# The first sequence of a spectral-mixing and SwiGLU kernel, by a written list of steps over eight PSUM banks

## The chip, the cores and the metric

The kernel runs on one core of a Trainium2 chip. The metric is the device time of one launch in microseconds; lower is better. The core has a matrix engine (PE, TensorE), three engines for elementwise work (DVE is VectorE, ACT is ScalarE, POOL is GpSimd), a fast memory (SBUF), eight banks of accumulators that PE writes (PSUM), and DMA queues. Each engine takes its instructions in the order in which they were written. In this kernel the queue of SP holds the intermediate stores, transposes and output stores, and the queue of POOL holds the loads of inputs and weights, between POOL's own arithmetic.

## The reference

Eight sequences of 3008 tokens with 256 channels are filtered in the frequency domain, and every token then goes through a normalised gated feed-forward layer:

```python
X = np.fft.rfft(x, axis=1)
Y = X * (filt_r + 1j * filt_i)[None]
y = np.fft.irfft(Y, n=3008, axis=1).reshape(-1, 256)
rms = np.sqrt(np.mean(y * y, axis=-1, keepdims=True) + 1e-06)
xn = y / rms * rms_g
g = xn @ w_gate                    # 256 x 1536
val = xn @ w_val
out = (g * (1 / (1 + np.exp(-g))) * val) @ w_out   # 1536 x 256
```

Inputs and output are float32; the kernel works with 16-bit floats in the matrix products.

## The kernel before

The transform of length 3008 = 47 * 64 is split in two matrix stages. For each sequence there are these steps, and each is a handful of matrix products into one PSUM bank followed by one instruction that moves the bank to SBUF:

- A (`a_unit`; `a0_unit` for the first sequence): the transform over 64. It needs a quarter of x (`x_load(b, c)`, four loads of six token groups each).
- B (`b_unit`): the transform over 47, sixteen units of 4 frequencies by 128 channels. Unit number 2g + dh holds frequencies 4g to 4g + 3 and channel half dh.
- The products with the filter (`s_part`): two per unit, both on DVE. The one with e = 0 multiplies by the real part of the filter, the one with e = 1 by the imaginary part, of which one half must have been negated before. Unit i needs the negated piece of its own four frequencies and its own channel half.
- The inverse transform over 47 (`bi_unit`), and over 64 (`n_unit`), the normalisation, and for each of 6 groups of 512 tokens twelve steps of the feed-forward layer (`gv` and `down`).

Sequences 1 to 7 are prepared while PE works on the feed-forward layer of the sequence before; a planner at the end of the function puts their steps into the slots between `gv` calls. The first sequence has nothing to hide behind. Its part, from the first line under `tc.manual_schedule()` to `first_norm()`, is the prologue, and the change is there. In it the filter must also be turned (`f_unit(i, f, dh)`: four 32-bit transposes and two copies into the table `ff`; i is which of three staged tiles of filter rows, f = 0 the imaginary and f = 1 the real part, dh the channel half), the A results are transposed on PE (`tr0_unit(g)`, one copy of 96 x 1024), and the products are turned and added on PE (`yt0_unit`, one copy of 96 x 512). `f_neg(k0, n, dhs)` on POOL writes the negated imaginary part for n frequencies from k0 on, `f_last` one special column. Everything is issued in program order on each engine.

Four staging tiles (the pool `stg`) hold, one after the other, the three tiles of filter rows `fst[0..2]`, the three tiles of gate and value weights (`w_load(q)`, two DMAs of 512 KB each, called `ws`) and later the tiles y. With four buffers, `w_load(0)` gets the fourth; `w_load(1)` and `w_load(2)` each need a tile of filter rows whose transposes are over. `w_load(0)` and `w_load(1)` stand at the front of POOL's list, before any `f_neg`. `w_gain(q)` on POOL scales the staged weights by `moe_rms_g` into `wg` and `wv`; `wo_load(q)` loads a third of `w_out`. Third q of the weights serves the feed-forward steps jt = 4q to 4q + 3.

Before the change the sixteen units run in a loop of one unit per turn, in the order `od`: B of one unit, its two products, the turning (`yt0_unit`) of a unit two places earlier, the inverse (`bi_unit`) of one four places earlier. B uses the banks mx and mb in turn, the turning the two buffers of psG and the inverse the two of psV. All eight `tr0_unit` copies are on DVE, all twelve `f_unit` copies on ACT, and nearly all turning and inverse copies on ACT.

After the loop come two A units of the second sequence, a small first group of transposes and the first normalisation (`t4_first`, `first_norm`), and four transposing DMAs of all of the first sequence on SP's queue (`t4_load`). A tiny copy on POOL, `seen`, waits for the second of these, and holds back the loads that stand behind it.

Of the kernel before, what the change touches and what calls it, by code (L numbers as in the profile page):

```python
# [1 line left out]

# [1 line left out]

# [16 lines left out]
P = 128  # L21
D = 256
B = 8
# [3 lines left out]
K2 = 32  # L27
# [74 lines left out]
def kernel(  # L102
# [31 lines left out]
    xnp = ctx.enter_context(tc.tile_pool(name="xnp", bufs=4))  # L134
    hp = ctx.enter_context(tc.tile_pool(name="hp", bufs=4))
    op = ctx.enter_context(tc.tile_pool(name="op", bufs=2))
    psG = ctx.enter_context(tc.tile_pool(name="psG", bufs=2, space=bass.MemoryType.PSUM))
    psV = ctx.enter_context(tc.tile_pool(name="psV", bufs=2, space=bass.MemoryType.PSUM))
    psO = ctx.enter_context(tc.tile_pool(name="psO", bufs=1, space=bass.MemoryType.PSUM))
    psM = ctx.enter_context(tc.tile_pool(name="psM", bufs=1, space=bass.MemoryType.PSUM))  # L140
    psB = ctx.enter_context(tc.tile_pool(name="psB", bufs=1, space=bass.MemoryType.PSUM))
# [44 lines left out]
            nc.gpsimd.dma_start(t.rearrange("p a d -> p (a d)"), src(N2, XC))  # L186
        st[b]["x"][c] = t

    def bank(i, name):
        pool, tag = ((psM, "mx"), (psG, "pg"), (psV, "pv"), (psB, "mb"), (psO, "po0"))[i]  # L190
        return pool.tile([P, 512], FP32, tag=tag, name=name)

    def copy(eng, out, in_, scale=None):
        if eng == "A":
# [16 lines left out]
        nc.sync.dma_start(dst, st[b]["t1"][c])  # L211

    def t2_tile(b, c):
        if b == 0 and c == 3:
            st[b]["t2"][c] = op.tile([KR, KC, D], FP16, tag="o3", name="t2o")
        else:
            st[b]["t2"][c] = t2p.tile([KR, KC, D], FP16, tag="t2", name="t2")
# [5 lines left out]
    def s_part(b, i, e, eng=None):  # L223
        eng = eng or nc.vector
        g, dh = divmod(i, 2)
        ps, s = st[b]["s"][i]
        fv = ff[:, dh, 4 * g:4 * g + 4, :]
        o = s[e].rearrange("p k (r q) -> p k r q", r=2)
        if e == 0:
            f1 = fv[:, :, 2 * SL:3 * SL].unsqueeze(2).to_broadcast([P, 4, 2, SL])  # L230
            eng.tensor_tensor(out=o, in0=ps, in1=f1, op=ALU.mult)  # L231
        else:
            f2 = fv[:, :, 0:2 * SL].rearrange("p k (r q) -> p k r q", r=2)
            eng.tensor_tensor(out=o, in0=ps[:, :, ::-1, :], in1=f2, op=ALU.mult)  # L234

    def b_unit(b, i, bk=3, e=0):
        g, dh = divmod(i, 2)
        ps = bank(bk, "psb")[:, 0:4 * KR]
        for k in range(4):
            kk = 4 * g + k  # L240
            nc.tensor.matmul(ps[:, ts(k, KR)], st[b]["t2"][kk // KC][:, kk % KC, ds(dh * P, P)],  # L241
                             wb[0:KR, kk, :], start=True, stop=True)
# [119 lines left out]
    def tr0_unit(g, eng):  # L362
        pool, tag = ((psO, "po0"), (psO, "po1"), (psM, "mx"))[g % 3]
        ps = pool.tile([KR, 4, 2, P], FP16, tag=tag, name="pst")
        for k in range(4):
            for dh in range(2):
                nc.tensor.transpose(ps[:, k, dh, :], va[:, dh, 4 * g + k, :], ident)  # L367
# [17 lines left out]
    def f_unit(i, f, dh, e):  # L385
        t = fst[i]
        ps = bank(1 + "AV".index(e), "psf").rearrange("p (a q) -> p a q", a=FR4)
        for a in range(FR4):
            nc.tensor.transpose(ps[:, a, :], t[:, f, a, ds(dh * P, P)], idf)  # L389
# [17 lines left out]
    def f_neg(k0, n, dhs=(0, 1)):  # L407
        for dh in dhs:
            nc.gpsimd.tensor_scalar(out=ff[:, dh, k0:k0 + n, 0:SL], in0=ff[:, dh, k0:k0 + n, SL:2 * SL],
                                    scalar1=-1.0, scalar2=1.0, op0=ALU.mult, op1=ALU.mult)  # L410

    def yt0_unit(i, eng, bk, ks=slice(0, 4)):
        g, dh = divmod(i, 2)
# [119 lines left out]
    def gv(b, m, jt):  # L533
        n = nq(b, m)
        xn = st[b]["xn"][m]
        parts = ((0, 2), (2, 4)) if (b, m, jt) in SPLIT else ((0, n),)
        sg = hp.tile([P, 512], FP16, tag="sg", name="sg")
        hh = hhs[(6 * JT * b + JT * m + jt) % 4]
        made = []
        for q0, q1 in parts:  # L540
            w = (q1 - q0) * P
            pg = psG.tile([P, 512], FP32, tag="pg", name="pg")
            pv = psV.tile([P, 512], FP32, tag="pv", name="pv")
            for ps, wt in ((pg, wg), (pv, wv)):
                for dt_ in range(2):
                    nc.tensor.matmul(ps[:, 0:w], wt[:, dt_, ts(jt, P)], xn[:, q0:q1, dt_, :],  # L546
                                     start=(dt_ == 0), stop=(dt_ == 1))
# [49 lines left out]
    def wo_load(q):  # L597
        nc.gpsimd.dma_start(wo[:, ts(q, JT // 3), :],
                            moe_w_out.rearrange("(jt p) d -> p jt d", p=P)[:, ts(q, JT // 3), :])

    def w_gain(q):
        cols = ts(q, DFF // 3)
        t = wst.pop(q)
        for k, dst in enumerate((wg, wv)):
            for dt_ in range(2):
                nc.gpsimd.tensor_scalar(out=dst[:, dt_, cols], in0=t[:, k, dt_, :],
                                        scalar1=gsb[:, dt_:dt_ + 1], scalar2=1.0,
                                        op0=ALU.mult, op1=ALU.mult)

    with tc.manual_schedule():  # L610
        nc.vector.memset(ss3[0], 0.0)
# [61 lines left out]
        f_unit(1, 1, 1, "A")  # L673
        f_unit(2, 0, 1, "A")
        b_unit(0, od[2], 4, 1)
        f_unit(2, 1, 0, "A")
        for p in range(3):
            s_part(0, od[p], 0)
        for p in range(UN + 3):
            if 3 <= p < UN:  # L680
                b_unit(0, od[p], (0, 3)[p % 2])
                s_part(0, od[p], 1)
            if p == 0:
                f_unit(2, 1, 1, "A")
                f_neg(4, 12, (1,))
                f_last()
                f_neg(0, 4)
                w_load(2)
                wo_load(0)
                f_neg(16, 16)  # L690
# [5 lines left out]
            if 2 <= p < UN + 1:  # L696
                yt0_unit(od[p - 2], "A", 1)
            if p == UN + 1:
                yt0_unit(UN - 1, "V", 1, slice(0, 2))
                yt0_unit(UN - 1, "A", 0, slice(2, 4))  # L700
            if 4 <= p < UN + 3:
                bi_unit(0, od[p - 4], "AV"[p == UN + 1], 2)
            if UN + 1 <= p < UN + 3:
                fill(1, 1)
        bi_unit(0, UN - 1, "V", 3, slice(0, 2))
        bi_unit(0, UN - 1, "A", 0, slice(2, 4))
        a_unit(1, 0, "A", 1)
        t4_first()
        a_unit(1, 1, "V", 0)
        fill(1, 3)  # L710
        for c in range(NXC):
            t4_load(0, c)
        nc.gpsimd.tensor_copy(out=seen, in_=st[0]["t4"][1][:, 0, 0:4])
# [171 lines left out]
```

## Time and profile before

| | before |
|---|---|
| median of 3 runs | 863.09 us (863.01 to 863.34) |
| the profiled execution's own time | 863.15 us |
| its span in the trace | 861.4 us |
| PE busy | 852.4 us (99%) |
| DVE / ACT / POOL busy | 557.2 / 612.4 / 297.8 us |
| granted TensorE clock | 0.999 |
| first `gv` product on PE | 43.38 us after the span's start |

In the rows below, the first number is the start in microseconds from the span's start, the second the length of the group, then engine, line, operation, output and input, the count, and in brackets the idle time before it with what ended it. Instructions of one engine overlap a little: a product of 0.55 us on DVE is followed by the next one after 0.465 us. Two steps of a group (x2) are shown as one row.

### The profile page before, as it was taken

What the parts mean: (1) busy time and instruction counts of PE and PEld (TensorE: products, weight loads), DVE (VectorE), ACT (ScalarE), POOL (GpSimd) and SP (SyncE); (2) the same over time, 40 slices, a digit from 0 to 9 for tenths busy, and PEclk for the clock granted to TensorE, in tenths of its full rate; (3) what the DMA queues carried; (4) which work ended last, traced back from release to release, by engine and by line L of the source; (5) the groups of instructions that cost most, each with busy time, mean ns of one, the idle gap of its engine ahead of it and who ended that gap; (6) DMA issues with size and microseconds to landing.
All of it is one profiled execution on the core that took longest, in us unless ns stands there. A gap on an engine that the chain in (4) does not pass through costs nothing.

```text
span 861.4 us, 17024 instructions
## 1 busy us (share of the span) xinstructions
PE 852.4 (99%) x6142; PEld 532.2 (62%) x6142; DVE 557.2 (65%) x926; ACT 612.4 (71%) x1339; POOL 297.8 (35%) x346
## 2 busy tenths in 40 slices
PE   8999999999999999999999999999999999999997
PEld 6755666566666666666666666666666666665664
DVE  5857655776666666666666676767666665555554
ACT  4986777787588756887577856888567765777443
POOL 5725742453144322534034430444123430132000
PEclk9999999999999999999999999999999999999999
DMA  9995778765975476656755548433564331521101
GB/s 283 270 204 124 150 164 168 139 130 121 197 137 129 121 150 111 151 107 147 139 127 113 132 98 180 108 87 101 131 127 93 97 70 42 124 54 49 62 25 50
DMA packets 198237, 107.98 MB, mean 125 GB/s; under 512 B 158566, under 2 KB 182520, under 8 KB 198152
## 3 DMA queue, kind: packets, MB, share of 16 engines
q1 hardware_dynamic: 189464, 85.52, 44.1%
q0 software_dynamic: 8544, 21.24, 12.7%
q8 instruction: 48, 0.79, 0.4%
q14 instruction: 37, 0.30, 0.1%
q10 hardware_dynamic: 144, 0.13, 0.0%
HBM read 45.78 MB, written 35.65 MB: 95 GB/s over the span
## 4 chain that ended last, share of the span: by engine, by line
PE 96%; DMA 1%; ACT 1%; DVE 1%; issue 0%; POOL 0%; POOLq 0%
PE po L563 28%; PE pg L546 28%; PE pv L546 28%; PE psb L241 3%; PE psi L285 3%; PE psn L314 2%; PE psa L206 2%; DMA fs<-in_filt_i_dram 1%; PE psy L418 1%; PE psf L389 1%; PE pst L367 0%; ACT sg L550 0%; POOL xc L186 0%; DVE s L231 0%; DVE hh L551 0%
## 5 line engine op out<-in xcount | busy, mean ns | idle before, releaser
L551 DVE TENSOR_TENSOR hh<-pv,sg 128x512 f16<-128x512 f32 (+2 forms) x578 | 391.5, 678 | 286.4 <-ACT sg L550 221.9
L550 ACT ACTIVATE sg<-pg 128x512 f16<-128x512 f32 (+2 forms) x578 | 337.4, 584 | 217.6 <-PE pg L546 213.4
L546 PE MATMUL pg<-xn,wg 128*128 128x512 f16 (+2 forms) x1156 | 338.1, 374 | 0.1
L546 PE MATMUL pv<-xn,wv 128*128 128x512 f16 (+2 forms) x1156 | 338.1, 374 | 0.0
L563 PE MATMUL po<-wo,hh 128*128 128x256 f16 x2256 | 332.7, 273 | 0.0
L563 PEld LDWEIGHTS <-hh 128*128 128x128 f16 x2256 | 213.4, 98 | 105.5 <-issue 0.6
L268 POOL TENSOR_TENSOR ss<-s,s 128x384 f16<-128x384 f16 x112 | 101.9, 911 | 273.2 <-DVE s L234 245.2
L546 PEld LDWEIGHTS <-wv 128*128 128x128 f16 x1156 | 112.9, 98 | 130.7
L546 PEld LDWEIGHTS <-wg 128*128 128x128 f16 x1156 | 111.4, 98 | 17.0 <-issue 0.3
L340 POOL TENSOR_TENSOR xt<-y,rho 128x1024 f16<-128x1024 f32 (+1 forms) x46 | 85.4, 1856 | 2.8
L322 ACT ACTIVATE junk<-y 128x256 f16<-128x256 f32 x180 | 74.3, 413 | 2.8
L231 DVE TENSOR_TENSOR s<-psb,ff 128x384 f16<-128x384 f32 x124 | 67.6, 547 | 0.7 <-ACT ff L195 0.6
L234 DVE TENSOR_TENSOR s<-psb,ff 128x384 f16<-128x384 f32 x124 | 67.6, 546 | 0.0
L195 ACT ACTIVATE uu<-psi 128x384 f16<-128x384 f32 (+1 forms) x127 | 61.6, 486 | 1.5 <-DMA out_dram<-o 0.5
L195 ACT ACTIVATE y<-psn 128x512 f32<-128x512 f32 (+1 forms) x95 | 55.7, 588 | 4.2
L285 PEld LDWEIGHTS <-yt 96*128 96x128 f16 x512 | 35.4, 97 | 26.7 <-issue 1.0
L332 POOL TENSOR_TENSOR rho<-u,mhalf 128x4 f32<-128x4 f32 (+1 forms) x46 | 46.5, 1010 | 3.8
L330 POOL TENSOR_SCALAR u<-ss 128x4 f32<-128x4 f32 (+1 forms) x46 | 8.9, 193 | 104.8 <-ACT junk L322 103.8
L195 ACT ACTIVATE t<-psa 128x512 f16<-128x512 f32 x70 | 41.4, 594 | 3.1 <-PE psa L206 1.7
L285 PE MATMUL psi<-wi,yt 96*128 96x96 f16 x512 | 42.9, 205 | 0.1
L241 PE MATMUL psb<-wb,t 96*128 96x96 f16 x480 | 40.1, 206 | 0.3 <-DVE s L234 0.2
L241 PEld LDWEIGHTS <-t 96*128 96x128 f16 x480 | 28.7, 97 | 12.8 <-DVE s L234 3.3
(101 smaller groups left out, 366.2 us busy)
## 6 DMA issues: line engine op xcount, KB each, us to landing
out_dram<-o SPq DMA_DIRECT2D x40, 512.0 KB, 3.6
xc<-in_x_dram POOLq DMA_DIRECT2D x31, 384.0 KB, 5.6
z_tmp<-t SPq DMA_DIRECT2D x28, 384.0 KB, 2.7
t<-z_tmp SPq DMA_DIRECT2D x28, 384.0 KB, 6.0
out_dram<-o SPq DMA_DIRECT2D x7, 384.0 KB, 2.7
fs<-in_filt_i_dram POOLq DMA_DIRECT2D x3, 512.0 KB, 10.8
fs<-in_filt_r_dram POOLq DMA_DIRECT2D x3, 512.0 KB, 11.2
ws<-in_moe_w_gate_dram POOLq DMA_DIRECT2D x3, 512.0 KB, 9.8
```

The lines of the kernel that those rows point to most:

```text
L195: nc.scalar.activation(out=out, in_=in_, func=AXT.Copy, **({} if scale is None else {"scale": scale}))
L231: eng.tensor_tensor(out=o, in0=ps, in1=f1, op=ALU.mult)
L234: eng.tensor_tensor(out=o, in0=ps[:, :, ::-1, :], in1=f2, op=ALU.mult)
L241: nc.tensor.matmul(ps[:, ts(k, KR)], st[b]["t2"][kk // KC][:, kk % KC, ds(dh * P, P)], wb[0:KR, kk, :], start=True, stop=True)
L268: nc.gpsimd.tensor_tensor(out=ss3[g % 3][:, :, dh, 0:KR], in0=s[0], in1=s[1], op=ALU.add)
L285: nc.tensor.matmul(ps[:, k, :], yt[0:KR, k, dh, :], wi[0:KR, 4 * g + k, :], start=True, stop=True)
L322: nc.scalar.activation(out=junk, in_=y[:, i, ts(u, D)], func=AXT.Square, accum_out=ss[:, 2 * i + u:2 * i + u + 1])
L340: nc.gpsimd.tensor_tensor(out=xt[:, 0:n, :], in0=y.rearrange("p a (u d) -> p (a u) d", u=2)[:, 0:n, :], in1=rho[:, 0:n].unsqueeze(2).to_br ...
L546: nc.tensor.matmul(ps[:, 0:w], wt[:, dt_, ts(jt, P)], xn[:, q0:q1, dt_, :], start=(dt_ == 0), stop=(dt_ == 1))
L550: nc.scalar.activation(out=sg[:, c], in_=pg[:, 0:w], func=AXT.Silu)
L551: nc.vector.tensor_tensor(out=hh[:, c], in0=pv[:, 0:w], in1=sg[:, c], op=ALU.mult)
L563: nc.tensor.matmul(po[s4 // 2][:, s4 % 2, :], hh[:, ts(s4, P)], wo[:, jt, :], start=(jt == 0 and s4 % 2 == 0), stop=(jt == JT - 1 and (s4 ...
```

## The change

- **Banks.** The tags of psG and psV become two tags with one buffer each (`pg0`, `pg1`, `pv0`, `pv1`), so that each step of the prologue can name any of the eight banks. The feed-forward steps still alternate between the two of each kind.
- **A written list.** The loop over units is replaced by the string `STEPS`. Each entry is one step and its bank. F is `f_unit` (three digits i, f, dh, and then the engine of its copies), T is `tr0_unit` (g and the engine), N is `f_neg` for 4 frequencies (dh and g), L is `f_last`, B is a unit's transform (`b0_unit`), P is one product (unit and e), Y is the turning, I the inverse, W, O, X and G are loads and weight scaling, Z a filler product.
- **Order.** The filter tile 0 is turned half at first (F001, F000) and its second half late (F010 in the middle, F011 last). The first five products of the list are imaginary ones (P6.1, P2.1, P3.1, P5.1, P4.1), which need negated pieces; before, the first three were imaginary ones also. Some copies change engine: those of T1, T2 and T5 move to ACT, those of F100, F010, Y13 and I10 to DVE, and that of I14 to ACT.
- **Six product buffers** in place of four: the two more are the tiles `hh0` to `hh3`.
- **Negation in sixteen pieces** of 4 frequencies and one channel half, each an instruction of 192 elements, in place of seven larger ones.
- **Loads.** `w_load(2)` stands after thirteen of the sixteen negated pieces; `x_load(1, 0)` and `x_load(1, 1)` stay in the prologue. `wo_load(1)`, `x_load(1, 2)` and `x_load(1, 3)` move behind `seen`, ahead of `wo_load(2)`. `w_gain` is called by halves (gate, value): three halves in the list, two more after `t4_load`, the last after the loads.

```diff
-    psG = ctx.enter_context(tc.tile_pool(name="psG", bufs=2, space=bass.MemoryType.PSUM))
-    psV = ctx.enter_context(tc.tile_pool(name="psV", bufs=2, space=bass.MemoryType.PSUM))
+    psG = ctx.enter_context(tc.tile_pool(name="psG", bufs=1, space=bass.MemoryType.PSUM))
+    psV = ctx.enter_context(tc.tile_pool(name="psV", bufs=1, space=bass.MemoryType.PSUM))
...
+    BANKS = {"mx": (psM, "mx"), "mb": (psB, "mb"), "o0": (psO, "po0"), "o1": (psO, "po1"),
+             "g0": (psG, "pg0"), "g1": (psG, "pg1"), "v0": (psV, "pv0"), "v1": (psV, "pv1")}
...
     def t2_tile(b, c):
-        if b == 0 and c == 3:
+        if b == 0 and len(st[b]["t2"]) == 3:
...
+    def b0_unit(i, bk, soft):
+        g, dh = divmod(i, 2)
+        ps = bank(bk, "psb")[:, 0:4 * KR]
+        for k in range(4):
+            kk = 4 * g + k
+            nc.tensor.matmul(ps[:, ts(k, KR)], st[0]["t2"][kk // KC][:, kk % KC, ds(dh * P, P)],
+                             wb[0:KR, kk, :], start=True, stop=True)
...
+        st[0]["s"][i] = (ps.rearrange("p (k r q) -> p k r q", k=4, r=2), s0_free.pop(0))
...
-    def w_gain(q):
+    def w_gain(q, k):
         cols = ts(q, DFF // 3)
-        t = wst.pop(q)
-        for k, dst in enumerate((wg, wv)):
-            for dt_ in range(2):
...
-        todo = [(i, f, dh) for i in range(2) for f in range(2) for dh in range(2)][:7] + [(2, 0, 0)]
-        for u in todo[0:2]:
-            f_unit(*u, "A")
-        for g in range(7):
-            tr0_unit(g, "V")
-            if g < 6:
-                f_unit(*todo[g + 2], "A")
-        f_neg(4, 4, (0,))
-        f_neg(8, 8, (0,))
-        UN = K2 // 2
-        od = [2, 4, 6, 3, 5, 7, 0, 1] + list(range(8, UN))
-        tr0_unit(7, "V")
-        for p in range(2):
-            b_unit(0, od[p], (0, 3)[p], 1)
...
-        for p in range(UN + 3):
-            if 3 <= p < UN:
-                b_unit(0, od[p], (0, 3)[p % 2])
-                s_part(0, od[p], 1)
-            if p == 0:
-                f_unit(2, 1, 1, "A")
-                f_neg(4, 12, (1,))
                 f_last()
-                f_neg(0, 4)
-                w_load(2)
-                wo_load(0)
-                f_neg(16, 16)
-                wo_load(1)
-                for c in range(3):
-                    x_load(1, c)
-                for q in range(3):
-                    w_gain(q)
...
+        STEPS = """
+            F001A:v0 F000A:o1 T2A:g1 T6V:g0 T3V:mx T1A:o1 T0V:v1 T7V:g0 F101A:g1 F100V:o1 F110A:o0 T4V:v0
+            F200A:g1 F010V:mx F201A:o0 B6:mb T5A:v1 N03 B2:o1 B3:mx N01 N11 F111A:g1 P6.1 P2.1 P3.1 B5:g0
+            F210A:v0 N12 B4:v1 N02 N13 N15 P5.1 P4.1 N06 P4.0 P2.0 F211A:o0 F011A:g1 Y4A:v1 B1:v0 Y2A:o0 L B7:g1
+            P6.0 P3.0 N07 I4A:o1 N10 N04 P1.0 Y3A:mx N14 P7.0 P7.1 Y6A:v1 I2A:mb B9:o0 B8:mx B0:g1 N00 W2 P5.0
+            P1.1 Y5A:g0 P9.1 O0 Y1A:o1 Y7A:v1 I3A:mb P8.1 B11:v0 N16 P8.0 I5A:mx P9.0 I6A:o1 B10:v1 P0.0 I1A:o0
+            P0.1 B12:g0 Y9A:mb Y0A:o1 N05 Y8A:o0 P11.0 P10.0 I7A:mb P11.1 B14:g1 N17 P12.0 Y11A:v0 P10.1 B15:o0
+            I0A:o1 B13:v1 I9A:mb P12.1 Y12A:mx P14.1 P14.0 X0 P13.1 P13.0 Y10A:o1 P15.1 P15.0 Y14A:v0 I12A:mb
+            Y13V:v1 I11A:g1 I14A:v0 Y15aV:g0 Y15bA:o1 I10V:o0 I8A:g1 I13A:mx X1 G0 G1 G2 I15aV:v0 Z1:mb I15bV:o1"""
+
+        s0_free = [[sp.tile([P, 4, KR], FP16, tag="s%d" % n, name="s%d" % n) for n in range(2)]
+                   for _ in range(4)]
+        s0_free += [[hhs[2 * i + n][:, 0:4 * KR].rearrange("p (k q) -> p k q", k=4) for n in range(2)]
+                    for i in range(2)]
...
         for c in range(NXC):
             t4_load(0, c)
+        w_gain(1, 1)
+        w_gain(2, 0)
         nc.gpsimd.tensor_copy(out=seen, in_=st[0]["t4"][1][:, 0, 0:4])
+        wo_load(1)
+        x_load(1, 2)
+        x_load(1, 3)
         wo_load(2)
-        x_load(1, 3)
+        w_gain(2, 1)
         first_norm()
```

More of the change, by code (lines that the diff above doesn't have):

```diff
@@ L1 @@
 from contextlib import ExitStack
+from functools import partial
 import numpy as np
@@ L187, in x_load, with bank @@
         st[b]["x"][c] = t
-    def bank(i, name):
-        pool, tag = ((psM, "mx"), (psG, "pg"), (psV, "pv"), (psB, "mb"), (psO, "po0"))[i]
-        return pool.tile([P, 512], FP32, tag=tag, name=name)
+    BANKS = {"mx": (psM, "mx"), "mb": (psB, "mb"), "o0": (psO, "po0"), "o1": (psO, "po1"),
+             "g0": (psG, "pg0"), "g1": (psG, "pg1"), "v0": (psV, "pv0"), "v1": (psV, "pv1")}
+    turn = {"g": 0, "v": 0}
+    def bank(i, name, shape=(P, 512), dt=FP32):
+        if not isinstance(i, str):
+            i = ("mx", "g", "v", "mb", "o0")[i]
+        if i in turn:
+            turn[i] += 1
+            i += "01"[turn[i] % 2]
+        pool, tag = BANKS[i]
+        return pool.tile(list(shape), dt, tag=tag, name=name)
     def copy(eng, out, in_, scale=None):
@@ L360, in a0_unit, with tr0_unit @@
              ps.rearrange("p (u t) -> p t u", u=4))
-    def tr0_unit(g, eng):
-        pool, tag = ((psO, "po0"), (psO, "po1"), (psM, "mx"))[g % 3]
-        ps = pool.tile([KR, 4, 2, P], FP16, tag=tag, name="pst")
+    def tr0_unit(g, eng, bk):
+        ps = bank(bk, "pst", (KR, 4, 2, P), FP16)
         for k in range(4):
@@ L383, in f_load, with f_unit @@
                                 raw(src, row, [[FR4 * D, P], [1, FR4 * D]]))
-    def f_unit(i, f, dh, e):
+    def f_unit(i, f, dh, e, bk):
         t = fst[i]
-        ps = bank(1 + "AV".index(e), "psf").rearrange("p (a q) -> p a q", a=FR4)
+        ps = bank(bk, "psf").rearrange("p (a q) -> p a q", a=FR4)
         for a in range(FR4):
@@ L410, in f_neg @@
                                     scalar1=-1.0, scalar2=1.0, op0=ALU.mult, op1=ALU.mult)
+    def b0_unit(i, bk, soft):
[5 more added lines that the diff above has]
+                             wb[0:KR, kk, :], start=True, stop=True)
+        if soft:
+            v = xnp.tile([P, 512], FP32, tag="xn", name="v0")[:, 0:4 * KR]
+            copy("A", v, ps)
+            ps = v
+        st[0]["s"][i] = (ps.rearrange("p (k r q) -> p k r q", k=4, r=2), s0_free.pop(0))
     def yt0_unit(i, eng, bk, ks=slice(0, 4)):
@@ L541, in gv @@
             w = (q1 - q0) * P
-            pg = psG.tile([P, 512], FP32, tag="pg", name="pg")
-            pv = psV.tile([P, 512], FP32, tag="pv", name="pv")
+            pg, pv = bank("g", "pg"), bank("v", "pv")
             for ps, wt in ((pg, wg), (pv, wv)):
@@ L599, in wo_load @@
                             moe_w_out.rearrange("(jt p) d -> p jt d", p=P)[:, ts(q, JT // 3), :])
-    def w_gain(q):
+    def w_gain(q, k):
         cols = ts(q, DFF // 3)
-        t = wst.pop(q)
-        for k, dst in enumerate((wg, wv)):
-            for dt_ in range(2):
-                nc.gpsimd.tensor_scalar(out=dst[:, dt_, cols], in0=t[:, k, dt_, :],
-                                        scalar1=gsb[:, dt_:dt_ + 1], scalar2=1.0,
-                                        op0=ALU.mult, op1=ALU.mult)
+        for dt_ in range(2):
+            nc.gpsimd.tensor_scalar(out=(wg, wv)[k][:, dt_, cols], in0=wst[q][:, k, dt_, :],
+                                    scalar1=gsb[:, dt_:dt_ + 1], scalar2=1.0, op0=ALU.mult, op1=ALU.mult)
     with tc.manual_schedule():
@@ L673 @@
[L673 to L678, printed above, removed]
-        for p in range(UN + 3):
-            if 3 <= p < UN:
-                b_unit(0, od[p], (0, 3)[p % 2])
-                s_part(0, od[p], 1)
-            if p == 0:
-                f_unit(2, 1, 1, "A")
-                f_neg(4, 12, (1,))
-                f_last()
-                f_neg(0, 4)
-                w_load(2)
-                wo_load(0)
-                f_neg(16, 16)
-                wo_load(1)
-                for c in range(3):
-                    x_load(1, c)
-                for q in range(3):
-                    w_gain(q)
[L696 to L704, printed above, removed]
@@ L705 @@
-        bi_unit(0, UN - 1, "V", 3, slice(0, 2))
-        bi_unit(0, UN - 1, "A", 0, slice(2, 4))
-        a_unit(1, 0, "A", 1)
+        STEPS = """
[7 more added lines that the diff above has]
+            Y13V:v1 I11A:g1 I14A:v0 Y15aV:g0 Y15bA:o1 I10V:o0 I8A:g1 I13A:mx X1 G0 G1 G2 I15aV:v0 Z1:mb I15bV:o1"""
@@ new lines @@
+        s0_free = [[sp.tile([P, 4, KR], FP16, tag="s%d" % n, name="s%d" % n) for n in range(2)]
+                   for _ in range(4)]
+        s0_free += [[hhs[2 * i + n][:, 0:4 * KR].rearrange("p (k q) -> p k q", k=4) for n in range(2)]
+                    for i in range(2)]
+        halves = {"": slice(0, 4), "a": slice(0, 2), "b": slice(2, 4)}
+        soft = set()
+        for step in STEPS.split():
+            head, _, bk = step.partition(":")
+            k, a = head[0], head[1:]
+            if k == "F":
+                f_unit(int(a[0]), int(a[1]), int(a[2]), a[3], bk)
+            elif k == "T":
+                tr0_unit(int(a[0]), a[1], bk)
+            elif k == "N":
+                f_neg(4 * int(a[1]), 4, (int(a[0]),))
+            elif k == "L":
+                f_last()
+            elif k == "B":
+                if a[-1] == "s":
+                    soft.add(a[:-1])
+                b0_unit(int(a.rstrip("s")), bk, a[-1] == "s")
+            elif k == "P":
+                u, e = a.split(".")
+                s_part(0, int(u), int(e), nc.gpsimd if u in soft else None)
+            elif k == "Y" or k == "I":
+                u = a[:-1].rstrip("ab")
+                (yt0_unit if k == "Y" else partial(bi_unit, 0))(int(u), a[-1], bk, halves[a[len(u):-1]])
+                if k == "Y" and a[len(u):-1] != "a":
+                    s0_free.append(st[0]["s"][int(u)][1])
+            elif k == "Z":
+                fill(int(a), bk)
+            elif k == "W":
+                w_load(int(a))
+            elif k == "O":
+                wo_load(int(a))
+            elif k == "X":
+                x_load(1, int(a))
+            elif k == "G":
+                w_gain(*divmod(int(a), 2))
@@ L708 @@
+        a_unit(1, 0, "A", "g0")
         t4_first()
-        a_unit(1, 1, "V", 0)
-        fill(1, 3)
+        a_unit(1, 1, "V", "mx")
+        fill(1, "mb")
         for c in range(NXC):
             t4_load(0, c)
+        w_gain(1, 1)
+        w_gain(2, 0)
         nc.gpsimd.tensor_copy(out=seen, in_=st[0]["t4"][1][:, 0, 0:4])
+        wo_load(1)
+        x_load(1, 2)
+        x_load(1, 3)
         wo_load(2)
-        x_load(1, 3)
+        w_gain(2, 1)
         first_norm()
```

## The prediction

> **What bounds the kernel now.** First the page: the busy shares and the chain that ended last.
>
> ```profile
> PE 852.4 (99%) x6142; PEld 532.2 (62%) x6142; DVE 557.2 (65%) x926; ACT 612.4 (71%) x1339; POOL 297.8 (35%) x346
> PE 96%; DMA 1%; ACT 1%; DVE 1%; issue 0%; POOL 0%; POOLq 0%
> ```
>
> PE is never idle once the feed-forward layer has begun, so the change is worth what it does to the start of the first `gv`, and what it does afterwards to PE's waits. Next, therefore, the timelines of the first 60 us, engine by engine. PE: the first filter transposes, the steps between them, an early A pair of the second sequence, and the first `gv`.
>
> ```profile
> 13.03 1.06 PE L389 MATMUL psf<-tab,fs 128*128 128x128 f32 x8 [0.40 <-DMA fs<-in_filt_i_dram]
> 14.41 0.66 PE L389 MATMUL psf<-tab,fs 128*128 128x128 f32 x4
> 18.90 0.61 PE L389 MATMUL psf<-tab,fs 128*128 128x128 f32 x4
> 20.24 0.51 PE L241 MATMUL psb<-wb,t 96*128 96x96 f16 x8
> 43.38 0.38 PE L546 MATMUL pg<-xn,wg 128*128 128x256 f16 x2
> 54.30 0.60 PE L206 MATMUL psa<-xc,tab 128*128 128x512 f16 x2
> ```
>
> DVE: the last A copies, then the products, the last product, and the last inverse copy.
>
> ```profile
> 12.22 1.29 DVE L197 CAST uu<-psa 128x512 f16<-128x512 f32 x2 [0.98 <-PE psa L357]
> 21.20 1.47 DVE L234 TENSOR_TENSOR s<-psb,ff 128x384 f16<-128x384 f32 x3
> 25.32 0.55 DVE L234 TENSOR_TENSOR s<-psb,ff 128x384 f16<-128x384 f32 x1
> 36.47 0.54 DVE L234 TENSOR_TENSOR s<-psb,ff 128x384 f16<-128x384 f32 x1
> 38.60 0.36 DVE L197 CAST uu<-psi 128x192 f16<-128x192 f32 x1 [0.18 <-PE psi L285]
> ```
>
> From 25.32 to 36.47 are 24 products, one per 0.465 us without a gap: the middle of the prologue goes at DVE's pace (and ACT's, which is as full). POOL: the second weight load, the negation behind it, and the loads behind `seen`.
>
> ```profile
> 18.59 0.70 POOL L594 DMA_DIRECT2D ws<-in_moe_w_gate_dram  x1 [0.83 <-PE pst L367]
> 19.28 0.72 POOL L594 DMA_DIRECT2D ws<-in_moe_w_val_dram  x1
> 20.28 0.84 POOL L409 TENSOR_SCALAR ff<-ff 128x192 f32<-128x192 f32 x2 [0.27 <-ACT ff L195]
> 46.02 0.18 POOL L713 COPY seen<-t 128x4 f16<-128x4 f16 x1 [6.64 <-DMA t<-uu]
> 46.15 0.80 POOL L598 DMA_DIRECT2D wo<-in_moe_w_out_dram  x1
> 46.94 0.61 POOL L186 DMA_DIRECT2D xc<-in_x_dram  x1
> 56.71 0.59 POOL L186 DMA_DIRECT2D xc<-in_x_dram  x1 [2.15 <-PE psa L206]
> xc<-in_x_dram POOLq DMA_DIRECT2D x1, 384.0 KB, 8.2
> ```
>
> The reader is to see that the negation stands in POOL's queue behind `w_load(1)`, and that a load of x issued behind `seen` and one `wo` load lands 8.2 us after its issue (last line, DMA issues from 46.8 to 47.1).
>
> **The change, part by part.**
>
> *When the first product can start.* `w_load(1)` needs a free staging tile. Before, that was filter tile 0, whose fourth turning had left PE at 15.96. In the new list tile 0 is finished last (F011), tile 1 before it (F111), so the load now waits for F111 on PE. F111 stands behind eight F, eight T and three B. F001 is first and uses v0, whose last A copy leaves DVE at 12.22 + 1.29 = 13.51, so it starts at 13.56 and not at 13.03. An F and a T together take 0.90 (14.41 to 18.90, five pairs); a B takes 0.17 (20.24 to 20.58 for two). 13.56 + 8 x 0.90 + 3 x 0.17 = 21.27; F111 itself ends 0.61 later, at 21.88. POOL reacts to PE with 0.30 of delay in the row at 56.71 (that PE step ended at 56.41): 22.18. The two issues take 0.70 and 0.72: 23.6. Then N03, 0.35 (the mean of three such pieces in the prologue's list of groups is 349 ns): 23.95, and P6.1, which needs it, at 24.0. DVE's order puts P6.1 and four more imaginary products first, so no real one can run meanwhile: DVE has nothing from about 20.7 (F010's copy) on. Before, the first product ran at 21.20. Bounds for POOL's reaction: 0.05 (compute steps on POOL start within 0.1 of what they wait for, as at 20.28 after an ACT copy that ended at 20.18) to 0.6 (the row at 18.59, 0.59 after the filter load of its other wait landed at 18.0, 11.7 after its issue at 6.30). So 23.75 to 24.3.
>
> *The products.* Still 32, all on DVE: 31 x 0.465 + 0.54 = 14.95. The last ends at 38.95 where it ended at 37.01. Two buffers more, eight banks and finer negation only help to keep the pace 0.465, which before's row already has; the pieces come every 0.33 (two in 0.66 at 24.04), faster than DVE takes them. Sixteen pieces cost POOL 16 x 0.33 = 5.3 in place of 0.84 + 0.67 + 0.66 + 1.65 = 3.8; `w_load(2)` is behind thirteen of them and is issued near 28.5 and not 24.65, and lands, with 6.5 to 7.0 as before, by 36.5, ahead of its first scaling near 42.
>
> *After the last product.* DVE has Y13 (0.61), half of Y15 (0.34), I10 (0.46) and two halves of I15 (0.28 + 0.36), each next to the other: 2.05 from start to end, the first starting 0.08 before the last product's end: 40.9; before, 38.96. The copies of F on DVE (no such row; the nearest are DVE copies of 256 elements from PSUM, 0.42) lie before 20.7, where DVE waits in any case. T on ACT has no row: by the line through ACT's 0.383 for 256 and 0.594 for 512 elements it is 1.02, at least 0.60 (ACT, 512 of 16 bits), at most 1.2; F100 needs T1's bank, which at 1.02 is free 0.1 before PE comes there, so at 1.2 it would cost 0.1 to 0.3 and at 0.6 nothing. ACT's first turning comes after the sixth product: 24.0 + 5 x 0.465 + 0.54 + 0.76 (from 23.85 to 24.61 before) = 27.6, and 14 Y at 0.49, half a Y 0.30 and 14 I at 0.385 are 12.55: 40.15, just inside DVE's 40.9. So the first `gv` goes from 43.38 to 45.3: **+1.9**. Bounds from the above: +1.2 (first product at 23.75, half a microsecond less in the tail because ACT and PE are ahead) to +2.7 (24.3, T dear, small waits between DVE and ACT).
>
> *The loads behind `seen`.* `x_load(1, 2)` was issued at about 30.6 and landed at 40. Now it stands behind `seen` and `wo_load(1)`, exactly where the row at 46.94 was: 8.2 after its issue. Its first user is the A pair at 54.30. Both move with the first normalisation (`seen` waits for a DMA of its result's tile), so the difference stays: 46.94 + 8.2 = 55.14 against 54.30, **+0.84** on PE, which has no slack there. Bounds: nothing, if it lands after 4.8 like the earliest x load, and 2.1, if after 9.5 like the last one of the prologue. `wo_load(1)` lands 6.0 after its issue, at 52.15 before the shift, and is needed at 53.00: hidden. Behind it `x_load(1, 3)` follows by 3.0 (384 KB took 52.15 to 55.14), at 58.1 against a need at 57.99 + 0.84, and `wo_load(2)` 2 later, 60.1 against 59.73 + 0.84: both hidden by under a microsecond. What is queued behind the load on POOL is the last `w_gain` (needed near 55, done near 50).
>
> [...] The row says 8.2, with transposes and stores on the same engines, and the sum goes by it.
>
> *The rest.* The alternation of psG and psV in `gv` is the same. `w_gain` halves lie in POOL's 6.64 us of idle before `seen`.
>
> **The sum**, against the profiled execution's 863.15 (the median of the runs shown is 863.09): 863.15 + 1.9 + 0.84 = 865.9.
>
> **The rivals.**
>
> *Loads in time.* The A pair finds its data: 863.15 + 1.9 = 865.05. For it: the load of x that landed at 40.0, beside the first of the four transposing DMAs, no longer runs beside them. Against: the 8.2 of the exact row.
>
> *Loads worse.* `x_load(1, 3)` and `wo_load(2)` have under 0.8 of cover, and the next x load in the row after took 5.3 for 384 KB (55.14 to 60.4) and not 3.0: up to 1.5 more, 867.4.
>
> *Not slower: DVE gets its first product early.* If POOL were not held (the negation right after F200, as at 20.28), the first product would start when F010's copy ends, 20.75; the last ends at 35.7, the tail at 37.75 and not 38.96: -1.2, and with the 0.84 the time is 862.8. It decides from a first product before 21.2. For it: the list's own order presumes N03 there. Against: POOL takes its queue in order, and 18.59 shows a load holding what follows.
>
> *A smaller loss:* the tail recovers more than I take from it, 864.2.
>
> **How the numbers follow.** 0.45 for the forecast (865.2 to 866.8), 0.24 for loads in time, 0.14 for loads worse, 0.09 for not slower, 0.08 for the smaller loss. 0.2% is 1.7 us, about what a measurement of this kernel tells from no change: below 861.4 is faster, above 864.8 slower. Not slower gives 0.06 to faster and 0.03 to the same, the smaller loss 0.07 and loads in time 0.05 to the same; the rest, 0.79, is slower. The range leaves out the not-slower case and half of the smaller loss below, and the worst of the loads above: 864.1 (+1.2 with loads in time is 864.35, less a little of the tail) to 868.0 (+2.7 and 2.1).
>
> **What would show it.** Right: POOL's second gate-weight load starts near 22 after an idle of some 4 us that PE's filter transposes ended; DVE idle from 20.7 to 24; 32 products at 0.465; the first `gv` at 45.3; one PE wait of 0.8 for x near 56. Wrong: a first product before 22, a product pace under 0.465, or `gv` before 44.

## The result and the profile after

The changed kernel takes 868.46 us, the median of four executions (867.64 to 868.75), and the kernel before beside it 863.18 (863.01 to 863.34): 5.28 us more, a ratio of 1.006 with a 95% interval of 1.0042 to 1.0077. The direction was as forecast; the forecast was 2.75 us more, and the median lies 0.46 us above the upper end of its range. The profiled execution took 868.75 us with a span of 867.0.

The page of the changed kernel first, busy shares and the chain that ended last:

```profile
PE 853.7 (98%) x6141; PEld 534.4 (62%) x6141; DVE 557.8 (64%) x929; ACT 612.7 (71%) x1336; POOL 299.2 (35%) x355
PE 93%; DMA 3%; ACT 2%; POOL 1%; DVE 1%; issue 0%; SPq 0%; POOLq 0%; DVEq 0%
```

PE gives 3 points of the chain to DMA, ACT and POOL, and its busy time is 1.3 us more for one matmul less: it did the same work more slowly somewhere. PE's timeline: a wait for a filter load, F111, the first turning, the first `gv`, the early A pair of the second sequence.

```profile
19.57 1.50 PE L398 MATMUL psf<-tab,fs 128*128 128x128 f32 x12 [0.51 <-DMA fs<-in_filt_i_dram]
21.87 0.62 PE L398 MATMUL psf<-tab,fs 128*128 128x128 f32 x4
27.66 1.09 PE L440 MATMUL psy<-tab,hh 128*96 128x128 f16 x8 [3.48 <-DVE hh L241]
48.41 0.38 PE L567 MATMUL pg<-xn,wg 128*128 128x256 f16 x2
59.88 0.61 PE L216 MATMUL psa<-xc,tab 128*128 128x512 f16 x2 [0.39 <-DMA xc<-in_x_dram]
```

F111 ends at 22.49. Then come the lines that matter most: PE idles 3.48 us before its first turning, and `gv` starts at 48.41 where it started at 43.38. POOL's timeline shows the hold that was forecast, and DVE's what the hold does to the products:

```profile
22.80 0.70 POOL L615 DMA_DIRECT2D ws<-in_moe_w_gate_dram  x1 [5.07 <-PE psb L426]
23.49 0.72 POOL L615 DMA_DIRECT2D ws<-in_moe_w_val_dram  x1
24.33 2.56 POOL L418 TENSOR_SCALAR ff<-ff 128x192 f32<-128x192 f32 x8
```

```profile
24.73 1.95 DVE L244 TENSOR_TENSOR s<-psb,ff 128x384 f16<-128x384 f32 x4 [3.31 <-POOL ff L418]
29.18 0.56 DVE L241 TENSOR_TENSOR hh<-psb,ff 128x384 f16<-128x384 f32 x1 [0.17 <-PE psb L426]
30.28 0.56 DVE L241 TENSOR_TENSOR hh<-psb,ff 128x384 f16<-128x384 f32 x1 [0.55 <-PE psb L426]
33.02 1.02 DVE L244 TENSOR_TENSOR s<-psb,ff 128x384 f16<-128x384 f32 x2 [0.79 <-PE psb L426]
40.93 0.54 DVE L241 TENSOR_TENSOR s<-psb,ff 128x384 f16<-128x384 f32 x1
```

The row of the hold names a B step (line 426) that follows F111 on PE; that it is F111 which the load waits for is tried in e9, where F111 alone is moved.

The products start at 24.73 and then wait for PE three times, where before 24 of them ran without a gap. Why PE was late is in its granted clock. The windows of 2 us give the window; its length; busy time (and instructions) of PE, PEld, DVE, ACT and POOL; the granted clock; DMA share and GB/s:

```profile
24.00:26.00 2.00, 0.18 (x2) 0.00 (x0) 1.27 (x3) 0.97 (x4) 1.88 (x7) 1.00 1.01 373
26.00:28.00 2.00, 0.34 (x3) 0.34 (x4) 2.00 (x6) 0.00 (x0) 2.00 (x8) 0.73 0.92 348
28.00:30.00 2.00, 2.00 (x24) 2.00 (x23) 1.56 (x4) 0.63 (x2) 2.00 (x5) 0.50 0.08 27
30.00:32.00 2.00, 2.00 (x24) 2.00 (x22) 1.72 (x4) 1.59 (x3) 1.98 (x6) 0.50 0.84 199
32.00:34.00 2.00, 2.00 (x28) 2.00 (x27) 1.21 (x4) 1.02 (x3) 2.00 (x5) 0.57 1.00 336
34.00:36.00 2.00, 1.92 (x40) 1.81 (x38) 2.00 (x6) 1.81 (x4) 2.00 (x4) 1.00 1.26 195
```

PE is all but idle from 24 to 28, and then runs some 24 matmuls in 2 us where it runs 40 at the full clock. In windows of half a microsecond the clock is 1.00 up to 26.5, 0.91 from 26.5 to 27, 0.50 up to 33.5, 0.77 in the next one and 1.00 behind it: half speed from 26.91 to 33.73, 6.8 us.

The 5.03 us by which `gv` is later, against the forecast's own terms:

| | before | forecast | after | after minus forecast's step |
|---|---|---|---|---|
| first product starts | 21.20 | 24.0 | 24.73 | +0.73 |
| the 32 products take | 15.81 | 14.95 | 16.74 | +1.79 |
| end of the last to the first `gv` | 6.37 | 6.35 | 6.94 | +0.59 |
| first `gv` | 43.38 | 45.3 | 48.41 | +3.1 |

Up to the A pair 0.55 us more is lost (59.88 - 54.30 = 5.58), 0.39 of it in the wait for x, and the whole execution is 868.75 - 863.15 = 5.60 longer.

### The profile page after: what moved, and what is told of

The parts are those of the page before. It is cut to its first block, busy times and chain, and to the rows that moved or that the text cites. A ratio compares the mean times of both kernels' runs of the same rounds, so it can differ in the third digit from the quotient of the medians.

```text
span 867.0 us, 17022 instructions
## 1 busy us (share of the span) xinstructions
PE 853.7 (98%) x6141; PEld 534.4 (62%) x6141; DVE 557.8 (64%) x929; ACT 612.7 (71%) x1336; POOL 299.2 (35%) x355
## 4 chain that ended last, share of the span: by engine, by line
PE 93%; DMA 3%; ACT 2%; POOL 1%; DVE 1%; issue 0%; SPq 0%; POOLq 0%; DVEq 0%
PE po L584 28%; PE pg L567 27%; PE pv L567 27%; PE psi L295 2%; PE psn L324 2%; PE psb L251 2%; PE psa L216 2%; DMA fs<-in_filt_i_dram 2%; DMA xc<-in_x_dram 1%; ACT yt L205 1%; DMA t<-uu 1%; ACT uu L205 1%; PE psy L440 0%; DVE hh L572 0%; POOL xc L187 0%
## 5 line engine op out<-in xcount | busy, mean ns | idle before, releaser
L244 DVE TENSOR_TENSOR s<-psb,ff 128x384 f16<-128x384 f32 x119 | 64.8, 547 | 4.1 <-POOL ff L418 3.3
L241 DVE TENSOR_TENSOR s<-psb,ff 128x384 f16<-128x384 f32 x119 | 64.8, 547 | 0.0
L205 ACT ACTIVATE uu<-psi 128x384 f16<-128x384 f32 x126 | 61.0, 493 | 1.1 <-PE psi L295 0.2
L251 PE MATMUL psb<-wb,t 96*128 96x96 f16 x432 | 36.2, 206 | 0.3 <-DVE s L244 0.3
L324 PE MATMUL psn<-t,tab 128*128 128x512 f16 x92 | 34.4, 374 | 0.1
```

The source lines that it names most:

```text
L205: nc.scalar.activation(out=out, in_=in_, func=AXT.Copy, **({} if scale is None else {"scale": scale}))
```

## The experiments

The theory after this trace: (1) the weight load that waits for F111 holds POOL and with it the negations, the products and the turnings; (2) the hold leaves PE idle for over 3 us, its clock is halved for a time, and the products wait for PE; (3) the late load of x costs up to a microsecond. The rivals: the order, the early imaginary products or the extra buffers cost time by themselves; or the hold costs all of it and the clock nothing.

The time each kernel shows in its profiled execution, and its median with the ratio to the kernel before on the same chip (863.2 to 863.3 in every comparison):

| run | first product | first `gv` | median us | ratio (95%) |
|---|---|---|---|---|
| before | 21.20 | 43.38 | 863.2 | 1 |
| changed kernel | 24.73 | 48.41 | 868.46 | 1.006 (1.0042 to 1.0077) |
| e1 load moved late | 20.95 | 43.82 | 863.91 | 1.0008 (0.9999 to 1.0018) |
| e2 gap filled | 24.67 | 46.07 | 872.29 | 1.0096 (1.0072 to 1.012) |
| e3 x early | 24.57 | 45.97 | 867.53 | 1.005 (1.0034 to 1.0065) |
| e4 before, held | 25.11 | 47.68 | 867.60 | 1.0053 (1.0036 to 1.007) |
| e6 as e1, x first | 20.88 | 42.47 | 863.61 | 1.0007 (0.9997 to 1.0017) |
| e7 the same program as e2, on another chip | 24.43 | 45.83 | 867.37 | 1.006 (1.0032 to 1.0088) |
| e8 as e4, gap filled | 25.20 | 46.69 | 866.01 | 1.0032 (1.002 to 1.0044) |
| e9 F111 early | 21.89 | 43.29 | 864.07 | 1.001 (1.0001 to 1.0019) |
| e10 as e9, x early | 21.96 | 43.36 | 863.14 | 0.9998 (0.9989 to 1.0007) |
| e11 load behind negations | 20.88 | 42.46 | 862.71 | 0.9993 (0.9984 to 1.0002) |

### The hold alone taken away (e1)

```diff
         w_load(0)
-        w_load(1)
...
-            ... B0:g1 N00 W2 P5.0
+            ... B0:g1 N00 W1 W2 P5.0
```

> The changed kernel with w_load(1) taken from the front of POOL's list and put just ahead of w_load(2), behind thirteen negated pieces; nothing else is changed. Theory of the hold (POOL, held by w_load(1) until F111 has left PE, starts the negation 4 us late; PE then idles for 3.5 us and runs at half clock until 33.7): the negation starts when F200 is copied, near 20.8, the first product near 21.2, the granted clock stays at 1.00, the 32 products take 15 us, first gv near 42.7, and with some 0.5 us of the wait for x left the time is 862.5 to 863.5. Rival, the list itself (its order, T copies on ACT, F and turning copies on DVE) costs the time: at least 866.

The first negation starts at 20.56 and the first product at 20.95; DVE has no gap among the products, the clock is 1.00 throughout, and 4.55 us of the 5.28 are back. That settles that most of the loss hangs on the place of one load. What is left, 0.4 us above the expected range, is new: with both weight loads ahead of them, the loads of x are issued at 31.05, and PE waits for the first of them.

```profile
20.56 0.68 POOL L418 TENSOR_SCALAR ff<-ff 128x192 f32<-128x192 f32 x2 [2.56 <-ACT ff L205]
20.95 2.10 DVE L244 TENSOR_TENSOR s<-psb,ff 128x384 f16<-128x384 f32 x4
39.28 0.38 PE L216 MATMUL psa<-xc,tab 128*128 128x512 f16 x1 [1.56 <-DMA xc<-in_x_dram]
```

### The late x, and the same idle time with and without the clock's drop (e3)

```diff
-            ... I13A:mx X1 G0
+            ... I13A:mx X1 O1 X2 G0
...
-        wo_load(1)
-        x_load(1, 2)
```

> The changed kernel with wo_load(1) and x_load(1, 2) back in the prologue, behind x_load(1, 1). Theory: PE's wait for x of 0.4 to 0.6 us near 59.9 goes and nothing takes its place, 867.9. Rival: the transfers queued behind become late instead, or the earlier loads delay the transposes that seen waits for: 868.5.

PE has no wait for x between 48 and 80. The median is 0.9 us lower, but the four times spread from 865.75 to 869.03, and the profiled one (865.75) shows why. PE idles the same 3.48 us, and the clock stays:

```profile
27.51 0.65 PE L440 MATMUL psy<-tab,hh 128*96 128x128 f16 x8 [3.48 <-DVE hh L241]
28.00:30.00 2.00, 2.00 (x41) 1.96 (x40) 2.00 (x5) 1.78 (x4) 2.00 (x5) 1.00 0.07 25
```

Here the 32 products take 14.95 us, from 24.57 to 39.52, and the first `gv` comes at 45.97. The mean granted clocks of the four executions are 0.999 (865.75 us), 0.998 (866.83), and 0.996 twice (868.22 and 869.03): time and lost clock go together. For the changed kernel itself they are 0.998 (867.64) and 0.996 three times (868.32 to 868.75). Only the profiled executions show the clock itself. 6.8 us at half speed take 0.004 off the mean of such a span, and 3.4 us 0.002; read by that, an estimate, the clock drops with the same wait in the program in most executions and not in all, and for different lengths. What decides it is not shown.

### The same hold in the order of before (e4), and with PE kept busy (e8)

```diff
+        for _ in range(4):
+            f_neg(16, 16, (0,))
         f_neg(4, 4, (0,))
```

> The kernel before, with four repeats of one negation (768 elements, 0.82 us each, same result) put on POOL ahead of its first negation, so that the old order is held by 3.3 us. Theory of hold and clock: first product near 24.5, PE idle for 3.5 to 4 us, granted clock 0.5 for some 6 us after it, and the time rises by more than the hold: 867.5 to 868.5. Hold without the clock's share: 866.4. Rival, the hold matters only in the new list: at most 864.5.

Four repeated negations hold POOL, and nothing else of the kernel before is touched. It becomes 4.4 us slower, nearly as slow as the changed kernel: the list of steps is not needed for the loss. PE idles 4.09 us, and its clock is 0.50 from 27.36 to 30.77 (by half-microsecond windows again: 0.86 from 27 to 27.5, 0.50 up to 30.5, 0.73 in the next one), 3.4 us where some 6 were expected:

```profile
27.12 0.90 PE L418 MATMUL psy<-tab,s 128*96 128x128 f16 x8 [4.09 <-DVE s L231]
28.45 0.56 DVE L231 TENSOR_TENSOR s<-psb,ff 128x384 f16<-128x384 f32 x1 [0.46 <-PE psb L241]
28.00:30.00 2.00, 2.00 (x24) 2.00 (x22) 1.46 (x3) 1.19 (x2) 1.98 (x3) 0.50 0.71 162
```

In e8 the same held kernel gets matmuls that compute nothing needed, in PE's idle time:

```diff
+            if p == 2:
+                fill(14, 2)
             if 2 <= p < UN + 1:
                 yt0_unit(od[p - 2], "A", 1)
```

> e4 (the order of before with POOL held by four more negations) with 14 filling matmuls of 128x512 ahead of the first Y step, in the 4.09 us for which PE idled. Clock theory: first product near 25.1, granted clock 1.00 from 24 to 32 (e4 0.92 and 0.65), no DVE idle of 0.4 us among the products, first gate product near 46.3 (e4 47.68), time 865.6 to 866.6 us against e4's 867.6. Rival (the loss of e4 is the hold alone, the clock costs nothing): 867.3 to 868.2 us, as e4.

```profile
27.21 0.65 PE L418 MATMUL psy<-tab,s 128*96 128x128 f16 x8 [1.10 <-DVE s L231]
28.00:30.00 2.00, 2.00 (x41) 1.96 (x38) 1.95 (x5) 1.90 (x4) 1.98 (x3) 1.00 0.67 156
```

The first product is no earlier (25.20), but the clock stays at 1.00, the products have no gap, `gv` is 0.99 us earlier and the median 1.6 us lower. So this hold of some 4 us costs 2.8 us (866.01 - 863.2) with the clock kept up and 1.6 us more when it falls.

### PE kept busy in the changed kernel (e7, and e2)

```diff
-            ... F011A:g1 Y4A:v1
+            ... F011A:g1 Z14:v0 Y4A:v1
```

> The changed kernel with nothing but 14 filling matmuls of 128x512 (0.22 us each, 3.2 us in e2) between F011 and the first Y step, in the time in which PE idled 3.48 us; loads as in the changed kernel. Clock theory: first product near 24.7 as before, granted clock 1.00 from 24 to 34, no DVE idle over 0.3 us among the 32 products, last product ended near 39.7, first gate product near 46.1, PE's wait for x 0.6 to 0.9 us near 57, time 866.0 to 867.0 us against 868.5. Rival (the idle of PE is not what stretched the products): the gaps in the products stay, time 868 us or more. If the products and the clock are as the clock theory says and the time is still 870 us or more, as most executions of e2 had it, then the filling matmuls cost something in a later stage, and the stage shows in the windows of 2 us.

Up to the first `gv` the clock theory holds to 0.3 us: clock 1.00, 32 products in 14.96 us, `gv` at 45.83 against 48.41. But only three of the six times (865.82, 866.16 and 866.22) are near where it put them; the others are 868.52, 869.71 and 874.05, and the median is above the expectation. The profiled one (868.52) shows where its time went, in ACT's and PE's timelines:

```profile
64.23 0.60 ACT L205 ACTIVATE t<-psa 128x512 f16<-128x512 f32 x1 [3.53 <-DMA z_tmp<-t]
64.88 0.38 PE L216 MATMUL psa<-xc,tab 128*128 128x512 f16 x1 [2.42 <-ACT t L205]
```

The first intermediate store of the second sequence was issued at 49.78, and the longest transfer of these stores and their reads took 14.4 us in this stretch (7.9 before, 9.0 in the changed kernel): 64.18, just when ACT's wait ends. ACT needs the store's tile again, and PE needs ACT. e2 is the same program, line for line, run before e7 on another chip:

> The changed kernel with 14 filler products put into PE's idle stretch behind F011; the hold of POOL stays. Theory of the clock (half of what the hold costs comes from PE's clock falling to 0.50 after the idle stretch): first product still near 24.7, granted clock 1.00 from 26 to 34, DVE's gaps of 0.17, 0.55 and 0.79 us gone, first gv near 46.4, time 866.0 to 866.8. Rival, the gaps come from the list's order on PE, where B stands behind the turnings: clock up, but the time within 0.5 us of the changed kernel's 868.5.

Its profiled execution (866.70) has the clock at 1.00, `gv` at 46.07, and a longest such transfer of 12.4 us, with ACT waiting 1.3 us for it; but eight of its ten times are between 869.8 and 875.4, so its median speaks against the expectation. Of the sixteen executions of this program, five took 865.41 to 866.70, as the clock theory has it, and eleven 868.52 to 875.37, no faster than the changed kernel. That late stores are the reason was seen in one of the eleven, the only one of them with a trace. Five of the eleven have a mean clock of 0.996, as the changed kernel with its 6.8 us at half speed: there the clock fell too, and no trace shows where. Nor is it shown why filling matmuls would make stores late. So filling did not make the changed kernel faster as a whole, and the price of the clock rests on the prologue of these traces, on e3, and on e4 against e8. e8, with the same filling in the other order, has none of the slow executions (865.25 to 866.57).

### One step moved (e9), and with it the loads (e10)

```diff
-            F200A:g1 F010V:mx F201A:o0 B6:mb ... N01 N11 F111A:g1 P6.1 P2.1 P3.1 B5:g0
+            F111A:g0 F200A:g1 F010V:mx F201A:o0 B6:mb ... N01 N11 P6.1 P2.1 P3.1 B5:g0
```

> The changed kernel with one step moved: F111, the last reader of the filter buffer that the second gate-weight load takes, stands right ahead of F200 (in bank g0) instead of ten steps later. All loads stay where the changed kernel has them. Hold theory: the load's wait for PE ends near 19 instead of 22.8 and only its wait for the landing of the filter load (2,0), near 19.5, is left, so POOL begins the negations near 21 instead of 24.33, the first product comes at 21.3 to 22.0 instead of 24.73, PE does not idle 3 us and its granted clock stays at 1.00 from 24 to 34, the first gate product comes between 42.8 and 43.6 (48.41), and the time is 862.8 to 864.0 us against 868.5: the whole loss from the place of one step of 0.45 us. Rival (the early imaginary products and the extra banks cost time by themselves): the first product comes at 21.5 but the first gate product stays over 44.5 and the time over 865.

```profile
19.94 0.71 POOL L615 DMA_DIRECT2D ws<-in_moe_w_gate_dram  x1 [2.10 <-PE psf L398]
21.89 1.95 DVE L244 TENSOR_TENSOR s<-psb,ff 128x384 f16<-128x384 f32 x4 [0.58 <-POOL ff L418]
43.29 0.38 PE L567 MATMUL pg<-xn,wg 128*128 128x256 f16 x2
55.56 0.61 PE L216 MATMUL psa<-xc,tab 128*128 128x512 f16 x2 [1.19 <-DMA xc<-in_x_dram]
```

With F111 ten places earlier the load goes out 2.9 us earlier, the products start 2.84 earlier, the clock never drops and 4.4 us are gone. What is left of the loss, 0.8 us, is in the last line: the wait for x that the prediction priced at 0.84, now 1.19.

> As e9, and the second third of the down weights and x(1,2) are back ahead of the scheduled part as in the kernel before, so that nothing of the second sequence's x waits behind the copy `seen`. If the late x still costs something once the hold is gone: 0.3 to 0.8 us under e9, no PE wait for x between 48 and 62, time 862.2 to 863.2 us, level with before (863.2) or up to 0.1% under it. If the late x is hidden: as e9.

With e3's edit of the loads as well, `gv` is where it was (43.36), the wait for x is gone, and the median falls by 0.93 us to 863.14, the time before. The two intervals overlap, so the 0.93 rests on the medians and on the wait that goes. Nothing measurable is left that the list, the early imaginary products or the six buffers would cost.

### A version without the hold (e6, e11)

e6 is e1 with the loads of x ahead of the weight loads and e3's edit:

> The second gate-and-value weight load stands behind the negations, as in e1, and the loads of the second sequence's x(1,0) and x(1,1) stand ahead of it; the second third of the down weights and x(1,2) are back ahead of the scheduled part. Hold theory (the hold of POOL is what the changed kernel loses, and e1's rest is its late x): first product near 20.9, x(1,0) issued near 26.4 instead of 31.05, no PE wait over 0.3 us for x near 39, first gate product between 42.3 and 43.1 (e1 43.82, before 43.38), time between 862.0 and 863.2 us, the level of before or just under it. Rival (the list of steps, the early imaginary products or the extra buffers cost something by themselves): the first gate product stays near 43.8 although the wait for x is gone, and the time stays at e1's 863.9 us or above.

`gv` comes at 42.47, earlier than in either kernel, and the time is still 863.61, above the expected range. The last of the weight loads, the second third of `w_out` and x(1,2) are issued at 29.57, 32.00 and 32.79, ahead of the transposing DMAs that start at 38.13: these take 11.00 us on SP's queue where they took 8.11 before, land up to 8.6 us after their issue (6.0 before), and PE waits 0.63 us for one. That the loads make them slow was not tried.

```profile
47.91 0.40 PE L505 MATMUL psn<-tab,t 128*128 128x128 f16 x4 [0.63 <-DMA t<-uu]
```

e11 puts the load where its buffer has just come free, behind the seventh negation:

```diff
-            F210A:v0 N12 B4:v1 N02 N13 N15 P5.1
+            F210A:v0 N12 B4:v1 N02 N13 N15 W1 P5.1
```

(with `w_load(1)` at the front left out, and e3's edit).

> The changed kernel with the second gate-and-value weight load (two POOL issues) moved from ahead of the listed steps to behind the first seven negations (22.8 by their pace of 0.33 us from 20.5), where F111 has just ended (22.49 in the changed kernel), and the second third of the down weights and x(1,2) back ahead of the scheduled part. If nothing but the place of the load and the late x costs time, this takes e1's early first product without e1's late loads: first product at 20.9 to 21.2 (e10 21.96, changed kernel 24.73), x(1,0) issued near 30 as in e10 (e1 31.05), no PE wait over 0.5 us for x near 39, four transposing reads of uu over about 8 us and not 11 as in e6, first gate product 42.4 to 42.8, time 862.0 to 862.8 us against 863.2 of the kernel before: 0.05 to 0.15% under it. Rival (what is won ahead of the first gate product is lost again to late transfers, as in e1 and e6): first gate product near 42.5 and time 863.2 to 864.

```profile
22.90 0.77 POOL L615 DMA_DIRECT2D ws<-in_moe_w_gate_dram  x1
42.46 0.38 PE L567 MATMUL pg<-xn,wg 128*128 128x256 f16 x2
59.87 0.60 PE L584 MATMUL po<-wo,hh 128*128 128x256 f16 x4 [0.56 <-DMA wo<-in_moe_w_out_dram]
```

The load no longer waits. The median of 862.71 is the lowest of all, 0.55 us under the kernel before beside it and 5.75 under the changed kernel; against before the interval still holds 1, so it is not shown to be faster. Of the 0.92 us won at `gv` a part goes to waits behind it (0.56 in the profiled execution, whose 863.32 is one of the longer times); the transposing DMAs take 9.5 us here, not the 8 expected.

## Why the prediction was right in kind and wrong in size

- **When the first product can start.** The mechanism was right, instruction by instruction: the load waits for F111, holds POOL for 5.07 us, and the negation and P6.1 follow at once. The time was 0.73 short: F111 ended at 22.49 and not 21.88, 0.51 of it because F200 waited for the filter load (2, 0), which landed 13.2 us after its issue (11.7 in the trace of before). The bounds were set on POOL's reaction alone, not on the DMA that feeds a step ahead of F111. Without that wait the first product came at 24.43 (e7).
- **The products: this is the step that failed.** "31 x 0.465 + 0.54 = 14.95" took PE's speed as given, and the upper bound allowed only for "small waits between DVE and ACT". They took 16.74. The text named DVE's idle time from 20.7 to 24, but not that PE behind it would have nothing to do from 24.2 on. From 26.91 on, still in that idle time, PE's clock was 0.50 for 6.8 us, and PE became the one that DVE waited for. With the clock at 1.00 the term is exact: 14.95 in e3, 14.96 in e7.
- **After the last product.** 6.94 instead of 6.35; 6.45 in e3 and 6.44 in e7. Some 0.5 us here too comes from the clock, through ACT's turnings, which started behind; the rest was 0.1 off.
- **The loads behind `seen`.** Priced at 0.84 with bounds of 0 and 2.1: 0.39 in the changed kernel, where `seen` came 2.28 us after the first `gv` and not 2.64 as before, 1.19 in e9, and 0.93 between the medians of e9 and e10. The row of 8.2 us was the right one to go by: in this stretch of the changed kernel x landed 7.6 to 9.7 us after its issue.
- **The sum and the rivals.** 865.9 is about what this order takes when the clock stays: 865.75 in one execution of e3 and 865.41 to 866.70 in five of the filled kernel. That it fits e3 so closely is luck: there `gv` came at 45.97, 0.67 later than forecast, and there is no wait for x, which is 0.84 in the sum. The rival "not slower" had its mechanism right as well: with POOL free the first product came at 20.88. That e11's 862.71 is near its 862.8 is luck too, for e11 has its loads early, and less the 0.84 the rival's time would be 862.0. "Loads worse", at 867.4, is not what made it slow. The right rival was missing: the hold with a drop of the clock, 865.9 plus about 2.3 (1.79 and 0.5), 868.2.

## What to carry to other kernels

A load that must wait for its buffer holds everything behind it in its queue, arithmetic included (here POOL for 5.07 us, and the negations with it): put it behind the work that others wait for, or finish the buffer's last reader earlier (here one step of 0.45 us, moved, was worth 4.4 us). And when a change delays one engine, follow the delay to PE: idle times of 3.48 and 4.09 us there were paid twice here, once as themselves and once as 6.8 and 3.4 us at half clock in the stage that came next, and one of 3.48 us in e3 was not. A stage's measured pace need not hold when PE's clock in that stage falls: the 32 products took 14.95 us at 1.00 (e3) and 16.74 with 6.8 us at 0.50.

## What the runs showed that was not expected

- Idle times of PE of about the same length cost differently. In the changed kernel PE was idle for 3.48 us, from 24.18 to 27.66; the clock fell at 26.91, 2.7 us into it, and was 0.50 for 6.8 us. In e4 PE was idle for 4.09 us, from 23.03 to 27.12; the clock fell at 27.36, when PE had begun again, and was 0.50 for 3.4 us. In e3 PE was idle for 3.48 us, from 24.03 to 27.51, and the clock stayed at 1.00; so it did in e7 and e8, where filling matmuls left 0.47 and 1.10 us of idle time ahead of the first turning. So the length of the idle time alone does not decide whether the clock falls, or for how long: e3 and the changed kernel have the same, and the 4.09 us of e4 had the shorter time at half speed. What decides was not shown, and no run moved the idle time or its length in small steps.
- A transfer of 384 KB between SBUF and memory took 4.6 to 7.9 us at this place in the kernel before and 4.6 to 9.0 in the changed one; one took 14.4 us in an execution of e7, and held PE for 2.42 us by way of ACT.
- What an earlier start won was lost again, in part or whole, to waits for transfers in all three versions that had it: 1.56 us in e1, 0.63 in e6, 0.56 in e11, each for another transfer. `gv` started 0.9 us earlier than before in e6 and e11, and the kernel ended 0.4 us later and 0.55 earlier.
